# Reciprocals through a DRAM scratch and transposes by DMA, in a two-layer attention and token-MLP kernel on one core

## The chip, the cores and the metric

One Trainium2 chip, one core. The metric is the device time of one execution in microseconds, as the median of several runs. The profile is of one execution, taken by the hardware profiler; its span leaves out a little at both ends.

## The reference

S = 2048 tokens of D = 512 values, bf16. Two layers, each with an attention part A and a token-mixing part B, with the same weights in both layers:

```python
def _A_ref(x, wqkv, wo):            # H = 32 heads of Dh = 16, window W = 256
    qkv = (x @ wqkv).reshape(B, S, 3, H, Dh).transpose(2, 0, 3, 1, 4)
    scores = einsum("bhqd,bhkd->bhqk", q, k) * Dh ** -0.5
    mask = (i - j >= 0) & (i - j < W)
    p = softmax(where(mask, scores, -1e9))
    return einsum("bhqk,bhkd->bhqd", p, v).transpose(0, 2, 1, 3).reshape(B, S, D) @ wo

def _B_ref(x, w1, b1, w2, b2):      # F = 1792; mixes over the tokens
    u = gelu(einsum("bsd,sf->bdf", _layernorm(x), w1) + b1)
    return (einsum("bdf,fs->bds", u, w2) + b2).transpose(0, 2, 1)

x = x + _A_ref(_layernorm(x), wqkv, wo)
x = x + _B_ref(_layernorm(x), w1, b1, w2, b2)
# and both once more
```

## The kernel before

**Tiling.** The 2048 tokens are 16 tiles of 128 rows (`x_sb[:, t]`, t = 0 to 15) and four blocks Q of 512 tokens. The 32 heads are four groups t of eight. A block's attention is 4 groups x 9 steps = 36 steps, so a layer has 144. In each step TensorE makes scores of 64 x 64 cells into one of two pairs of PSUM banks (`emit_scores`, L689), ScalarE takes the exponent (`emit_exp`, L700), VectorE or GpSimd multiplies the edges of the window with a triangle mask (L717), and TensorE multiplies with V (`emit_pv`, L738), which also sums the denominators through two columns of ones. Beside the steps of a block run its own and the next block's projections.

**From x to Q, K, V.** A norm is statistics on VectorE (`ln_stats`, L509 and L510), then `ln_apply`: variance plus epsilon (L517), a pow on GpSimd (L519), the shift (L523), and the scaled tile `xh_sb` on VectorE, ScalarE or GpSimd (L526, L529). `job_transpose` turns a tile of `xh_sb` with four matmuls against the identity into PSUM (L549) and copies it to `xhT` (L433 on VectorE, L435 on ScalarE); `xhT` has two buffers for blocks. `job_k` and `job_q` project (`project`, L560), `job_v` too (L605); `masked` (L570 on VectorE, L575 on ScalarE) copies the result out of PSUM, spread over two masks.

**Denominators.** When a group is done, its outputs and denominators are copied to `oU` and `o2`; after two groups, four small DMAs collect the denominators into `den_c` (one row of 128 for each part of a head), and one larger DMA joins `o2` to `oU`. `job_inverse` takes the reciprocal (L763) and splits it into two bf16 parts `rc2` (L765 to L768). `job_normalise` spreads each reciprocal over the rows of its head with 32 small matmuls against `spread` (L781), two calls for a block, and VectorE multiplies (L788) into `oT`. `job_outproj` multiplies with wo (L654) and adds to x (L658). All this is done for a block while the next block's steps run, and for the last block after the attention.

**B.** `job_part` (L847) and `job_u` (L879) make the hidden layer, gelu on ScalarE (L886); `job_y` (L898) makes one tile of the output and adds it to x (L902), or in the last layer stores it. Most of layer 0's `job_y` runs beside layer 1's attention.

**Order.** Every operation is written down once with its reads and writes; `Plan` derives the waits. The order on each engine is not found at build time: packed tables (`ORDER`, `BANKS`, `LINES`) hold it, so each engine runs its own fixed list and stops at an operation whose inputs are not there. All loads and stores but two go through SyncE's list, also in order; many weight loads wait there for a certain exponent, so that they do not start too early. The costs in the operations were used to make the tables and do nothing at run time.

Of the kernel before, what the change touches and what calls it, by code (L numbers as in the profile page):

```python
# [10 lines left out]
P = 128  # L11
# [17 lines left out]
def _table(*text):  # L29
# [5 lines left out]
    'c-p;`jShq`2!r`}|A)TQnCSkPh09?~oC4CWo!JqbH)hxBetJf`ng_zSzB^KWCUz4<bw1?zP(^V@1hjoFX{LB!YpY$}WrX*L{g9dTE!G)(6{W?M'  # L35
    '{=Ja?K~YUKU36cs_mkwz6jZcU1~NAclX%DtfnKsWV;$C9+@DkPj_>@+4?Xa<j?hPIj3%PZW{uqQCtvU50|dGNd;')
ORDER = _table(
    'c-jrrgMttU00qE@tj)G<d$VoZwz=81ZQHhO+jiZ}M+`s+;b8<rC<I4Hgg_VsAS|LIG$JAj!XXACAsV70GUA{iVj(6XATDAf5#k{}5+E^>A|a9^'
    '1(M((QXv^qA`Ma_EwUpUG9Vo?Av4M%BeEhV(xV8nAUAR#7xEx4@}mIiA`pd96$McUCD0VbPzuFS1|?A%<xl}dQ3+Mh0p(E<)lnI>kPkIb4Rufx'
    'wb32*(HPy(0QJxejnD#3&>XGM8bi<$ZP6ZW&;y;(4xP{uUC<T%&<lMq2|Y0Yz0ntg(H~1O8UryALoo;=5QG^RhEW)fu^5Rl7>_xafT<XV>6nZu'  # L40
    'n2l+eg}IoAnb?PgSb)V?h80+Z<yeI!SdFz<i8a`O`B;a|*o5`iijCNT$Jm11*p6M;i*4A6L)e1@*pI_Ff@3(2qd18ZID@mefKxb+bGU@lxQdIo'
    'g6p`98+e3=xP_azhP$|j+qi@Kcz~z)fR}iICwPYEc#ZFPg?IP}5`2qKc#m)Rj4z1Ig#3Xw$iiRvihuZtzlg&>_>JHU#b6B0kTk<F1j8~S!!Uqi'
    'ct&Lu#$ZfFVmwA;1SViC#$|j)XCfwHWF}@ICSy{jWOAlwYNld3reGRoWLjomX69rzW@1+6V0PwWKIUa^mSG+SGCvEjDvPrqi?J|^upx`GG)u4~'
    'yR#Ncu`J86BFnQfE3g_{uo7#q3hS~u>##N(us)lx5$mxgTeC5nu_;@zGn=y|+p-NiuoDNeJv*`sd$Sw+uq%6U5PPs6d$KPFa2SI)hW$B&LphwI'
    'Ig;}@f}=QrV>yoFIg!&ig_Agyvp9p(Ig<-Hm$SKmOWBT#IiHKTgsZrmD>#{}xr{5hfonO3gSmz~xt=$;k(+p(o4JlRxrNubk9)b5w|Ix!c$c@i'
    'i@Ujl+qs7ad4Oklh^M)qXL*^&d6MUOiYIuEM|hOSc!h^~i5Ga0_j!+xc$H82jL-RsFZh@b`G7C^iBI^JZ}^(;_<^4pO&|H5Klz1U`JKP`jnr@c'
    '<qukM^oPMEg;X&8`#*y)3ZZZct*{EE07X)GMN|aEQ(Q$?WJOUb#Z*+qRt&{bd?iqNB~c<JRAQx5G9_0ErBoW_R6(UyCZ$zAWl=_DP<CZiW@S@S'
    '<y8*lRxagH0Tohy1**6TtB8uJs7k4<N~)YnsEn$pqDrg0DyXU|tEMWcx~i#;YN(!StCs4js~W3;nyS8fsF8ZBxtgez+N-sisjXUSoI0qDI;ovH'
    's-gO*v%0CLx~q#?XpnlTzeZ`G`YA{QG)#jvQhha4BQ!>%HC_`mRTDKyQ#4uAHBGZMQ*$&|GqhY|HD8M~PfN5=L$p}Sv`Q<rMk};b!?jlHwLqJ+'
    'P8+pZTeMnRwO!k^Q#&+EN3}=$v|D?1M7MQNhqXcbbwDR{NT;<+$Mi_YbxId?R_Am@Cv`@bbX6C0U6*xD!F*Hq^jLp&M>q6Pw{%wz^g{RbM$hzG'  # L50
    '&-GIA{YvNcRB!c8pY&Og{ZZfbP4D$Zzf{0KME}!o{ge&=ksQJy{XwA}&Y>LOCko?8j^Kz6?<kJyBo6NAj^S92=Gac<c#h))PUyJK=EM%`<WA~D'
    'PU&Qh>90!R^iJ(GPUj5H;*8GZCQj=z&g#t0?d;Cs>dxa_F6ewN>YUE&LeB3JF5+SibZM7#ahG>tmvUKGaXD9VMOSqNS95(=c1_oC9oKVP*LEW}'
    'a9uZdQ#W)gH+D0(bQ`yDJ9l(z*K!AUa%XpOSGV^7_i%6bba(f1U-xl;_wxu3_8<p&hzEL@hq{}`dbr1Uq$hf`$9tS7c$z1Bl&5&Qr+SWOc#>y&'
    'r4M<j4|=v|`LO4Dp6C0BS9yUK`luKAxR3dSmwAa7d%0J5tyg=ycX*xGc&B%Ho40tY_j<GUd6U<Bk2iXQ_j|Vw__ELXnos(MZ~206`?^p0lCSup'
    'ullA>`;71SoX`7-AN#%^`JwOmfuH%VpZbNL`#%hy?#l')
LINES = {
    "tensor": _table(
    'c-jTQ2fPS$9suzF@BiDz#|qDk(4ms8+^dL-yT_R!XJqdcITE2qR(bY%vNDS2!$bB6Wn}b(%l52{r#zR29QXZ}3Z=s{p-d<n%7tgcUqbm%Ayf>{'
    'g~ae`s1sffZ9@I<Mraq_3mw9g&^9E8&f$YFD@+O#!iOOxObx@r(l9g34-3MguqrGGYr?v)GOP~iVN2K;wukRSM%Wv6hXdhY$OA{i>98mK8P0_x'
    ';Z!&qE``hCdbkm)!=3P3C<V8}&jFx02;_tS3^^bl6oCJQ1SkQ0p)izz3Q!!bhRW~^l!q5!G}MB|FbY~iO=tvfK{IFr9iSsDfUeLJy1-Z%2tA-b'  # L60
    '42BW#F^q$Wunkfm879CSm<m^6HEe-}uncCyd^i9rVJWPI6_5t$a11uV9@q~%U^jdV``|ESzzHZB&%znF1lQpvT!bItF5H8MkOlYQ37i6r7#~C4'
    'm@~#WAr^``VxCwq7K;U9)mSu^jx}Sgm>6G+wPU^bdQ6IqVvE=`Hi>OwgV;W{j_qQv*gKAo$+3Uz7vGIT<2!M991|zUC2>YfiId{gI6JP7v*N<I'
    'EbfhaVroo_i{q;JdCZQF<MX&F?u={V#<(s1Hy(<|Vn#d_55yz!WV{g1$Nlj}ydJaS-S}%f6aS14;=>rwF*7#7+?WdsVqPqbMKA$NVm>U3C9n)u'
    'z*_hsmd8q19joEXSP$!9BKE^Z_!>6AhBzMEU=p^#mbe&uVQcJ)-S9Y0$DTL<2jVE4frD`@4#f#L1k-Q|j=^y_2PflfT#Ko=06)W}xDi+3N?eZz'
    'a2;;NFL4hZ#Qm6wyKx_$#w&OPui>|N3N!E=p2f?UjdxHe3-94Ci1Y-j&?C%Ek&LR6Q!dI&#VLXEQ86k<MW{5DqO$Z71*$|9s0P)c9hgXs=&$q|'
    'HK2y{6xE{+ltj&_BK?R>sXcX~&eVnG(M(!LpVBN^O>3w>&8GD<h|*~)jifP@Lc?eXrO`B6M2l%YEubZ|i8j!ew3en*DjlVrG>5j*Hp-ww^cC%*'
    'uW2uRL&xYUU8KWwf^O3_x<lD?pDs~k<OD9kIoY`gE9d5XJe&)0e$K-+xg=NQ=eaV!#FhB(oXB;#Iyd5p+>Bds9Zuq={5PJ&4Y)J6=Qp_>cjC6('
    'oBMG$?#tadg+JjDJcx(z8XnE#co=`c$vmBB@E%^sb9oM@avJaArM!$+@+wZ}lYEQ!^ESTB$9XRw=7W5U7xQ`k51-~tKF2pWi?8z?e#G}Un}6pA'
    'jFMlTFi9zS%=x6K6qW>ePM(%$rJPigno?0-luA-V21rAxD@pRQyen_WP#G<6N)!2qye;kIpVCs+NoVOH|B{Z<UFyqN=`DlgJ$Xm^NOPGgBV~dt'
    'mnkw`K9UtOS?0+!St7|YR~E}^`9jiVgZwOC%VyakJLR5imqT(;PD_TIk+pJGj>tv1CP(F#T#&0WOK!?f0vc5Gkz`4#xaQVODX6*hDNWEKN?Ke?'  # L70
    'Ybh<KW%YzK)~Z@lt7r{P(&74wHq^XYTNAalHrG1ZL_gB5+Duz%J8iGMw5|5hE;>+q>Hz&lhv-P1s9QBz2kZMfMyKgKovkT4Q^6K!s(z-+^_H&H'
    'G;L`cb(e0}eY!z+>Rvsh8M;_c=><KhS9G%epf@yAuj?Jn(%hD<_w_gZU5nadeWYk&wJnF8(E?W3-16H4{anjhAuDN5TNztwHLS8#u>qE3)h*Fp'
    'v1F@ft*ohavO3np+FA?iZgs7*4Ys$ek9D)&HpoWWF#ETSwlOxxCfayQvAH(NQf;QKx2cwHD{O`>u+_H6mfIJ$&NkW(n_}B-k9}qP?TBr*YxcdJ'
    'vD0?Key|I6-ZJg7J+v&lWA`lEZrTI;#g3c#AIARJZdqRc&T@Hi&*^!*u!ARfB`@ZsynvVX=)L>}ui{m`ns@XO{<e4W_kFbY_Wu5=cl7~Y*ZX*5'
    'Z|L=Xj5qVK-p#xFNFV5ZeVkA9@!rD+`6M6ZvwWU+_78oUPxpmB-#_+GeTjeKvwf-W^UZ$95Bq*k^PRrdclj1y@9BQrPx&ps?l=6Lf9Iz?)3g1q'
    'U-8@ilb`oL{DJ@K5B<LXAER~eNB'),
    "vector": _table(
    'c-jrli&qF{6aeu1-S6J}-OrhZ%A=5XMS13N$}@^$X(h(YW7*EO)-;BRGxJCz;fyo02V%!;Oxv<ep2u;pt#gL340~0|G8whDVXxm`@M{Ml5DM*~'
    '0|Y`#Xam8}7MeqA2!a4;1^uBf^oA(t1N|Tx20#o9f*}wK!(bFlfE0KHl3^T-ha{K?sgMSRuoN<25@bRF3^!|Fgc)iUL%bPjhM67E4NKt=d=5RZ'
# [946 lines left out]
```

## Time and profile before

The runs took 512.4 to 515.64 us, with a median of 514.01. The profiled execution took 514.23 us; its span is 512.1 us.

| | busy us | share of the span |
|---|---|---|
| PE (TensorE matmul) | 481.0 | 94% |
| DVE (VectorE) | 314.1 | 61% |
| ACT (ScalarE) | 323.2 | 63% |
| POOL (GpSimd) | 196.6 | 38% |
| scores L689, PV L738 | 106.5, 90.8 | |
| exponents L700 | 262.8 | |
| transposes L549 (128 matmuls), spread L781 (512) | 11.8, 10.5 | |
| copies of transposes L433, products L788 | 12.4, 20.6 | |

Stages, in us of the span: start to the first score 0 to 17.3; attention of layer 0 to 170.4; B of layer 0 to 243.6; attention of layer 1 to 421.0 (with the rest of layer 0's B in it); B of layer 1 to 512.1. The granted TensorE clock is 1.0 throughout.

How to read it: the chain that ended last goes back from the last instruction, at each step to what released it. A group's line gives line, engine, operation, output and inputs, count, then busy time and mean of one in ns, then the idle time just before and what ended it. In a line of the timeline the first two numbers are the start and the duration in us.

### The profile page before, as it was taken

What the parts mean: (1) busy time and instruction counts of PE and PEld (TensorE: products, weight loads), DVE (VectorE), ACT (ScalarE), POOL (GpSimd) and SP (SyncE); (2) the same over time, 40 slices, a digit from 0 to 9 for tenths busy, and PEclk for the clock granted to TensorE, in tenths of its full rate; (3) what the DMA queues carried; (4) which work ended last, traced back from release to release, by engine and by line L of the source; (5) the groups of instructions that cost most, each with busy time, mean ns of one, the idle gap of its engine ahead of it and who ended that gap; (6) DMA issues with size and microseconds to landing.
All of it is one profiled execution on the core that took longest, in us unless ns stands there. A gap on an engine that the chain in (4) does not pass through costs nothing.

```text
span 512.1 us, 21417 instructions
## 1 busy us (share of the span) xinstructions
PE 481.0 (94%) x9532; PEld 273.9 (53%) x9624; DVE 314.1 (61%) x600; ACT 323.2 (63%) x387; POOL 196.6 (38%) x402
## 2 busy tenths in 40 slices
PE   7889999999999999999899999999899999999997
PEld 3556656665555444445555565666555554444443
DVE  5689878888454661367665764988773754431213
ACT  2989899899999404313678877888888880240000
POOL 5787764856344410010444533664353440100000
PEclk9999999999999999999999999999999999999999
DMA  6192211241121553140003200014213165042632
GB/s 205 47 86 66 69 44 59 78 121 35 36 74 52 157 150 99 47 137 10 4 3 97 86 16 26 4 46 118 76 46 106 47 171 164 12 132 85 193 102 72
DMA packets 70587, 40.71 MB, mean 79 GB/s; under 512 B 7008, under 2 KB 69472, under 8 KB 70496
## 3 DMA queue, kind: packets, MB, share of 16 engines
q1 hardware_dynamic: 66624, 39.33, 26.0%
q0 software_dynamic: 3872, 0.02, 1.5%
q8 instruction: 75, 1.23, 1.0%
q14 instruction: 16, 0.13, 0.1%
HBM read 32.51 MB, written 2.10 MB: 68 GB/s over the span
## 4 chain that ended last, share of the span: by engine, by line
PE 74%; DVE 10%; ACT 7%; issue 4%; POOL 3%; DMA 1%; SPq 0%; POOLq 0%; ACTq 0%; DVEq 0%
PE ps L898 17%; PE ps L689 11%; PE ps L879 11%; PE ps L738 9%; PE ps L560 8%; ACT p_sb L700 5%; PE ps L847 5%; PE ps L605 5%; PE ps L654 4%; DVE stats L509 2%; POOL p_sb L717 1%; PE ps L549 1%; DVE v_all L570 1%; DMA w1buf<-in_B_w_dram 1%; DVE oT L788 1%
## 5 line engine op out<-in xcount | busy, mean ns | idle before, releaser
L700 ACT ACTIVATE p_sb<-ps 128x1024 bf16<-128x1024 f32 (+7 forms) x288 | 262.8, 973 | 41.6 <-PE ps L689 33.9
L717 POOL TENSOR_TENSOR p_sb<-p_sb,edge 128x64 bf16<-128x64 bf16 (+2 forms) x301 | 141.6, 476 | 155.6 <-ACT p_sb L700 129.4
L689 PE MATMUL ps<-q_sb,k_sb 64*64 64x288 bf16 (+8 forms) x2816 | 106.5, 250 | 4.9 <-ACT p_sb L700 2.7
L738 PE MATMUL ps<-p_sb,v_all 64*34 64x288 bf16 (+17 forms) x2816 | 90.8, 245 | 1.7 <-POOL p_sb L717 0.8
L689 PEld LDWEIGHTS ps<-q_sb,k_sb 64*64 64x64 bf16 x2816 | 54.9, 106 | 49.5 <-ACT p_sb L700 25.8
L738 PEld LDWEIGHTS ps<-p_sb,v_all 64*34 64x34 bf16 (+1 forms) x2816 | 59.1, 100 | 14.5 <-POOL p_sb L717 5.1
L898 PE MATMUL ps<-ubuf,w1buf 128*128 128x512 bf16 x266 | 61.9, 379 | 2.7 <-DVE p_sb L717 1.3
L560 PE MATMUL ps<-xhT,wqkv 128*128 128x512 bf16 x214 | 56.5, 380 | 6.7 <-issue 4.6
L902 DVE SCALAR_TENSOR_TENSOR x_sb<-ps,b2col,x_sb 128x512 bf16<-128x512 f32 x32 | 23.7, 750 | 51.9 <-PE ps L898 51.2
L879 PE MATMUL ps<-xh_sb,w1buf 128*128 128x512 bf16 x186 | 43.1, 379 | 1.2 <-issue 0.6
L898 PEld LDWEIGHTS ps<-ubuf,w1buf 128*128 128x128 bf16 x280 | 26.1, 98 | 33.0 <-issue 2.8
L509 DVE BATCH_NORM_STATS2 stats<-x_sb 128x6 f32<-128x512 bf16 x64 | 43.0, 685 | 0.8
L519 POOL TENSOR_TENSOR rstd<-vare,mhalf 128x4 f32<-128x4 f32 x16 | 16.2, 1014 | 69.0 <-DVE vare L517 37.0
L529 ACT ACTIVATE xh_sb<-x_sb,shift,rstd 128x512 bf16<-128x512 bf16 x12 | 9.8, 817 | 48.2 <-POOL shift L523 37.8
L570 DVE TENSOR_TENSOR q_sb<-ps,even 128x1024 bf16<-128x1024 f32 x27 | 32.8, 1216 | 9.2 <-PE ps L560 8.1
L898 PE MATMUL ps<-ubuf,oU 128*128 128x512 bf16 x166 | 38.1, 379 | 0.1
L717 DVE TENSOR_TENSOR p_sb<-p_sb,edge 128x64 bf16<-128x64 bf16 (+2 forms) x99 | 24.4, 249 | 20.1 <-ACT p_sb L700 13.6
L886 ACT ACTIVATE ubuf<-ps,b1col 128x512 bf16<-128x512 f32 x28 | 18.7, 686 | 27.7 <-DVE ps L884 20.2
L570 DVE TENSOR_TENSOR k_sb<-ps,half 128x1024 bf16<-128x1024 f32 x27 | 32.9, 1218 | 5.1 <-PE ps L560 4.7
L605 PE MATMUL ps<-wqkv,xhT 128*32 128x128 bf16 x2048 | 33.9, 220 | 1.1 <-issue 1.1
L570 DVE TENSOR_TENSOR v_all<-ps,even 128x1024 bf16<-128x1024 f32 x26 | 31.6, 1217 | 5.6 <-PE ps L605 5.3
L560 PEld LDWEIGHTS ps<-xhT,wqkv 128*128 128x128 bf16 x256 | 20.6, 97 | 26.5 <-issue 4.2
(70 smaller groups left out, 462.7 us busy)
## 6 DMA issues: line engine op xcount, KB each, us to landing
w1buf<-in_B_w_dram SPq DMA_DIRECT2D x30, 256.0 KB
w1buf<-in_B_w_dram SPq DMA_DIRECT2D x50, 128.0 KB
oU<-in_B_w_dram SPq DMA_DIRECT2D x18, 256.0 KB
oU<-o SPq DMA_DIRECT2D x16, 256.0 KB
w1low<-in_B_w_dram SPq DMA_DIRECT2D x32, 128.0 KB
xhT<-in_B_w_dram SPq DMA_DIRECT2D x4, 512.0 KB
k_sb<-in_B_w_dram SPq DMA_DIRECT2D x4, 512.0 KB
out_dram<-x_sb SPq DMA_DIRECT2D x16, 128.0 KB
```

Of the source, the lines that this page charges most:

```text
L509: dve(lambda e: e.bn_stats(stats[:, t, :], x_sb[:, t, :]), 690, prio, reads=[R("x", t)], writes=[R("stats", t)])
L560: last = e.matmul(ps[:, b, :], lhsT=wqkv[:, c, c0:c0 + P], rhs=xhT[:, buf, c, :], start=(c == 0), stop=(c == 3))
L570: return e.tensor_tensor(dst, src.unsqueeze(2).to_broadcast([P, n, 2, w]), mask[:].unsqueeze(1).unsqueeze(3).to_broadcast([P, n, 2, w]), o ...
L605: last = e.matmul(acc[32 * a:32 * a + 32, k], lhsT=xhT[:, buf, c, t0:t0 + 32], rhs=wv[:, c, :, a, :], start=(k == 0 and c == 0), stop=(k = ...
L689: last = e.matmul(ps[64 * c:64 * c + 64, 2 * half + r, 32 * i0:32 * i1], lhsT=k_sb[rows, ring, t, kb % 16, :], rhs=q_sb[rows, t, c, 32 * i ...
L700: exps[plan.job] = last_exp[0] = plan.op({ACT: (170 + int(2 * (512 - c0) * 0.84), lambda e: e.activation(p_sb[:, slot, :, c0:512], ps[:, 2 ...
L717: return e.tensor_tensor(v, v, g, op=ALU.mult)
L738: last = e.matmul(ps[64 * r:64 * r + w, B_O + (c ^ r), 32 * i0:32 * i1], lhsT=v_all[rows, pos - 32 * c:pos - 32 * c + w], rhs=p_sb[rows, s ...
L847: r = e.matmul(ps[:, b, :], lhsT=w1low[:, fb % 2, sc, (ft % 2) * P:(ft % 2 + 1) * P], rhs=xh_sb[:, sc, :], start=(sc == 0), stop=(sc == 7))
L879: r = e.matmul(ps[:, b, :], lhsT=blk[:, sc - 8 * part, (ft % 2) * P:(ft % 2 + 1) * P], rhs=xh_sb[:, sc, :], start=(sc == 8 * part), stop=( ...
L898: r = e.matmul(ps[:, b, :], lhsT=blk[:, turn[n], (st % 2) * P:(st % 2 + 1) * P], rhs=u_at(turn[n]), start=(n == 0), stop=(n == NFT - 1))
L902: dve(lambda e: e.scalar_tensor_tensor(x_sb[:, st, :], ps[:, b, :], b2col[:, st:st + 1], x_sb[:, st, :], op0=ALU.add, op1=ALU.add), 750, prio,
```

## The change

Eight edits in one:

- For blocks 0 to 2 of each layer the reciprocal (fp32) goes by a DMA to a scratch in DRAM, `recip`, and comes back by four DMAs, `job_scale`, each of which repeats a head's row over its 16 partitions, into one of three buffers `rcb`. VectorE or GpSimd multiplies from there. The last block keeps the matmuls. The rows of `den_c` are in a new order.
- For blocks 1 to 3 of each layer the transposes are DMAs on SyncE's list, straight from `xh_sb` to `xhT`. Block 0 keeps TensorE.
- The first norm is done in two halves of two tiles, with the first x tiles loaded one by one, and its tiles go to VectorE or ScalarE.
- The first K and Q projections of each layer are done in halves of 256 columns.
- The last output tile is computed, added and stored in halves of 256 columns.
- A first exponent on a small tile is run ahead of everything.
- A part of `ln_apply` in layer 0's B gets its own place in the list of jobs.
- New tables, made with some other costs: the whole order on every engine is new. Among others the edge masks on VectorE go from 99 to 141 and on GpSimd from 301 to 259.

```diff
+        recip = nc.dram_tensor("recip", (P, P), dt.float32, kind="Internal").ap()
+        rcb = sb("rcb", [P, NRC, 512], dt.float32)          # NRC = 3
...
-        for t in range(0, 4, 2):
-            load_x(t, t + 2)
+        for t in range(4):
+            load_x(t, t + 1)
...
+        dve(lambda e: e.memset(touch[:], 0.0), 70, -101, writes=[R("touch")])
+        plan.op({ACT: (1480, lambda e: e.activation(touch[:], touch[:], ACTF.Exp))}, reads=[R("touch")], writes=[R("touch")], prio=-101)
...
         def job_transpose(Q, i, prio):
-            b, t, buf = misc_bank(), 4 * Q + i, Q % 2
+            t, buf = 4 * Q + i, Q % 2
+            if Q > 0:
+                plan.op({SP: (1250, lambda e: e.dma_start_transpose(xhT[:, buf, :, i * P:(i + 1) * P], xh_sb[:, t, :]))},
+                        reads=[R("xh", t)], writes=[R("xhT", buf, i)], prio=prio, dma=(1 << 17) + 1)
+                return
+            b = misc_bank()
...
+        def project_halves(Q, which, c0, banks, prio):
+            buf = Q % 2
+            for h, b in enumerate(banks):
+                def f(e, h=h, b=b):
+                    for c in range(4):
+                        last = e.matmul(ps[:, b, 0:256], lhsT=wqkv[:, c, c0:c0 + P], rhs=xhT[:, buf, c, 256 * h:256 * h + 256],
+                                        start=(c == 0), stop=(c == 3))
+                    return last
+                pe(f, 436, prio, reads=[R("wqkv", which)] + [R("xhT", buf, i) for i in (2 * h, 2 * h + 1)], writes=[BK(b)])
...
-                for t in range(2):
-                    todo.append((p0 + NORM0 + 1.4 * t, lambda p, t=t: job_normalise(Q - 1, t, p)))
+                for t in range(4):
+                    todo.append((p0 + NORM0 + 0.7 * t, lambda p, t=t: job_scale(Q - 1, t, p)))
...
             dve(lambda e: e.reciprocal(rc[:], den_c[:]), 930, prio, ...)
+            if Q < NQ - 1:
+                load(recip[:], rc[:], 1 << 16, prio, reads=[R("rc")], writes=[R("recip")])
+                return
...
+        def job_scale(Q, t, prio):
+
+            buf, n = Q % 2, t % NRC
+            row = recip[64 * (t // 2):64 * (t // 2) + 1, :]
+            src = bass.AP(tensor=row.tensor, offset=row.offset + 512 * (t % 2), ap=[[8 * P, 8], [0, DH], [1, 512]])
+            load(rcb[:, n], src, (1 << 18) + 1, prio, reads=[R("recip")], writes=[R("rcb", n)])
+            f = lambda e: e.tensor_tensor(oT[:, buf, t, :], oU[:, buf, t, :], rcb[:, n, :], op=ALU.mult)
+            plan.op({DVE: (640, f), POOL: (1300, f)}, prio=prio, reads=held_o(buf, t) + [R("rcb", n)], writes=[R("oT", buf, t)])
...
+            if last_layer and st == NT - 1:
+                for h, b in enumerate((3, 4)):
+                    cs = slice(256 * h, 256 * h + 256)
...
+                    load(out_v[:, st, cs], x_sb[:, st, cs], 1 << 16, prio, reads=[R("last", h)])
+                return
```

What the new order makes of it, in instructions: matmuls of L549 128 to 32, of L781 512 to 128; copies to `xhT` on VectorE 30 to 6; products into `oT` on VectorE 32 to 25 (17 of them from `rcb`) and 7 on GpSimd; SyncE's list 254 to 311 entries. On ScalarE 10 to 4 K halves, 10 to 4 Q halves and 11 to 4 copies to `o2`; 28 of those on VectorE, where 21 were.

## The prediction

> **What bounds the kernel now.** I read the totals and the chain that ended last, then the busy time by stage, then the waits, then the groups that the change touches. From the page:
>
> ```profile
> PE 481.0 (94%) x9532; PEld 273.9 (53%) x9624; DVE 314.1 (61%) x600; ACT 323.2 (63%) x387; POOL 196.6 (38%) x402
> PE 74%; DVE 10%; ACT 7%; issue 4%; POOL 3%; DMA 1%; SPq 0%; POOLq 0%; ACTq 0%; DVEq 0%
> ```
>
> TensorE is busy for 94% of the span and makes 74% of the chain; DMA has 1% of it. The windows cut at the first and last score matmul of each layer (PE, PEld, DVE, ACT, POOL) show the two attention stages:
>
> ```profile
> 17.30:170.40 153.10, 143.63 (x4098) 91.87 (x4132) 115.64 (x203) 139.68 (x162) 91.63 (x187) 1.00 0.29 69
> 243.60:421.00 177.40, 165.70 (x4190) 101.87 (x4232) 122.82 (x236) 145.49 (x172) 83.21 (x167) 1.00 0.20 58
> ```
>
> In layer 0 TensorE has 94% and ScalarE 91%: two bounds, nearly equal. In layer 1 it is 93% against 82%: TensorE alone. Each layer has 144 score steps, so one takes 153.1/144 = 1.06 us and 177.4/144 = 1.23 us; I use steps as a clock below. The waits of ScalarE in the two stages (total, times, longest) are for TensorE:
>
> ```profile
> ACT p_sb L700 <- PE ps L689: 9.1, 21, 0.8
> ACT p_sb L700 <- PE ps L689: 23.6, 35, 1.9
> ```
>
> **What leaves TensorE.** The groups of the transposes (L549) and of the reciprocal spread (L781), and how they stand in the stream:
>
> ```profile
> L549 PE MATMUL ps<-ident,xh_sb 128*128 128x128 bf16 x128 | 11.8, 220 | 2.6 <-ACT xh_sb L529 1.2 <-ACT v_all L575 0.7 <-ACT xhT L435 0.6
> L781 PE MATMUL ps<-rc,spread 64*64 64x128 bf16 x512 | 10.5, 218 | 0.8 <-DVE rc L768 0.4 <-issue 0.3
> ```
>
> ```profile
> 346.75 0.39 PE L549 MATMUL ps<-ident,xh_sb 128*128 128x128 bf16 x4
> 347.06 0.42 PE L689 MATMUL ps<-q_sb,k_sb 64*64 64x64 bf16 x12
> ```
>
> 24 of the 32 calls of four transposes go, and 12 of the 16 calls of 32 spread matmuls. A transpose call is busy for 11.8/32 = 0.37 us; the next work starts 0.31 us after it here. A spread call is busy for 0.65 us; between neighbours of its own kind the next starts 0.45 us later, so I take 0.5. That is 24 x 0.37 = 8.9 and 12 x 0.5 = 6.0 us, 14.9 in all, half in each attention stage: 7.4 each. In layer 1, where nothing else is near the bound, I count 6.5 of 7.4. In layer 0 ScalarE limits: by the two orders its own list shrinks by one masked V pair (2 x 0.69), two norm applies (2 x 0.82) and takes 1.0 us more of copies, 2.0 us less in all, and the rest can only come out of its waits. I take the middle of 2.0 and 7.4: 4.7.
>
> **VectorE and GpSimd** get no longer, so they cost nothing: VectorE loses 24 copies of 415 ns (10.0), 24 products from PSUM at 0.68 against 17 from SBUF at about the same (4.8), and takes 42 more edge masks of 0.25 (10.5) and 7 copies of 0.68 (4.8): about zero, at 75% and 69% busy in the two stages. GpSimd gives the 42 masks away (20 us) and takes 7 products, which no row shows: between 0.43 us (a quarter of the size) and four times that, 12 us at most.
>
> **What is added on SyncE's queue**: 24 transposing DMAs, 6 stores of the reciprocals (64 KB) and 24 loads of 256 KB. Rows for a DMA's price, from the timeline and the queues:
>
> ```profile
> 173.93 1.29 SPq L427 DMA_DIRECT2D den_c<-o  x2
> 176.66 0.95 DVE L763 RECIPROCAL rc<-den_c 128x128 f32<-128x128 f32 x1 [1.23 <-DMA den_c<-o]
> ```
>
> ```profile
> q1 hardware_dynamic: 66624, 39.33, 26.0%
> q0 software_dynamic: 3872, 0.02, 1.5%
> ```
>
> Issue takes about 0.6 us, and the last tiny DMA had landed 176.66 - 175.22 = 1.44 us later. A packet costs 0.26 x 512.1 x 16/66624 = 32 ns of one engine, whether it carries 590 bytes (first row) or 5 (second). So 57 more DMAs (three of them from the loads and stores that are split) of 0.6 us add 34 us to a queue whose long rows are gated waits: hidden, as long as what they bring is not late.
>
> *Transposes.* Not in this trace. Low end: a plain 128 KB, 256 packets of 512 bytes, 0.5 us. High end: cut into 32-byte pieces (16 rows of two bytes), 4096 x 32 ns/16 = 8.2 us (cut into single elements it would be 131 us; I leave that out as no use at all). I take 1 us of transfer and 2 us to land, nearest to the plain load of the same size. By the new order, from the issue of a block's set to the first use of its last member there are, in layer 0, 12 steps for four (12.7 us), 12 for three (12.7) and 15 for four (15.9); in layer 1, 16 (19.7), 18 (22.1) and 12 for four (14.8). All are covered, so cost 0. What covers them is that the norms of a block are finished a block ahead. Behind a transpose that waits for its norm on SyncE stand weight loads, whose uses come a stage later.
>
> *Reciprocals.* From the reciprocal to the first product: issue 0.6, land 1.44, issue 0.6, 256 KB at 18.5 GB/s (590 bytes in 32 ns) on 16 engines 0.89, land 1.44: 5.0 us. The new order leaves 6, 5 and 5 steps in layer 0 (6.4, 5.3, 5.3) and 5, 5 and 6 in layer 1 (6.2, 6.2, 7.4). It just fits; cost 0, but thin. The waiting product stands on VectorE (17) or GpSimd (7) ahead of copies out of PSUM and of edge masks, for which TensorE waits. The load's source has an outermost dimension of 8; if only 8 engines move it, 0.89 becomes 1.77 and the two gaps of 5.3 are missed by 0.6 each. The Trainium skill says just that ("DMA: Bandwidth & Descriptors", Rules for kernel authors: the slowest dimensions set how many engines take part, so an outermost dimension under 16 confines the DMA to that many); no run here shows it. By it the forecast is about 1 us longer.
>
> **Start.** The change loads ScalarE's table early, halves the first norm, K and Q, and puts V behind them:
>
> ```profile
> 8.67 1.28 ACT L529 ACT_TABLE_LOAD   x1 [8.67 <-POOL shift L523]
> ...
> 15.99 1.26 ACT L575 ACTIVATE q_sb<-ps,even 128x512 bf16<-128x512 f32 x2
> ...
> 18.28 1.90 ACT L700 ACTIVATE p_sb<-ps 128x960 bf16<-128x960 f32 x2
> ```
>
> The table's 1.28 us goes from the path. Of the halved norm I expect little, since the second half's pow (1.0 us on GpSimd) follows the first's. The first score now waits for two V calls on TensorE (1.04 each) and two Q masks on VectorE (0.65 each) side by side, where three ScalarE pairs of 1.26 stood in a row; but the first exponent still stands behind two V pairs on ScalarE. Bounds: 1.0 (the table, less two more matmul fills) to 3.5 (table, one V call and one mask). I take 2.0.
>
> **End.** The last output in halves shortens the 0.75 us of VectorE behind the last matmul to 0.41 by its halved columns, and the last store by at most 0.2:
>
> ```profile
> 508.93 0.02 issue
> 508.95 0.75 DVE x_sb L902
> ```
>
> Its 28 matmuls of 256 columns take what 14 of 512 took. I take 0.5.
>
> **Sum.** 2.0 + 4.7 + 6.5 + 0.5 = 13.7 us off the profiled execution's 514.2 (span 512.1, 2.1 around it; the median of the runs is 514.0): 500.5.
>
> **Rivals.** *(a) ScalarE bounds both stages*: its own lists shrink by 2.0 in each. For: 91% in layer 0, and the score slots tie the two engines together. Against: 82% in layer 1, with 23.6 us of waits for TensorE. With the start and the end as above: 514.2 - 2.0 - 2.0 - 2.5 = 507.7.
>
> *(b) The transposes are late: slower.* With T per transpose, one after another, the sets are late by what 4T (or 3T) exceeds the gaps above. At 8.2 us: 20.1 + 11.9 + 16.9 + 13.1 + 10.7 + 18.0 = 91, so 591. TensorE would stand at the V matmuls (L605 before) behind them. It decides from about T = 4.7, where the lateness eats the 13.7. For: 32 ns per packet however small. Against: nothing says that the pieces are that small. The Trainium skill ("VectorE: DVE Perf Modes", The three transpose paths) has 1309 ns for 128x128 by DMA against 390 ns on TensorE; the trace has four in 0.39 us busy on TensorE, and no DMA one. If four squares followed one another, 5.2 us, an estimate, the lateness would be 25 us and the time 525; if they overlap, nothing changes.
>
> *(c) The reciprocals are late*: each chain takes 8 us in place of 5.0. Late by 1.6 + 2.7 + 2.7 + 1.8 + 1.8 + 0.6 = 11, so 512. For: six serial chains through DRAM, margins of 0.3 us. Against: 4 to 6 steps lie between most products and their output projection.
>
> *(d) The new table leaves new holes* as large as the work removed: 514.
>
> **Chances.** Forecast 0.55, (a) 0.14, (b) 0.13, (c) 0.13, (d) 0.05. A measurement of this kernel tells about 1%, 5 us. Faster by more: the forecast, most of (a) and a little of (c), 0.70. Within: the rest of (a), half of (c) and of (d), 0.12. Slower: (b) and what is left, 0.18. Low end 489: the full 7.4 in both stages, 3.5 at the start, the 3.4 us of idle time in front of the two groups, and some of VectorE's waits behind them (7.1 at L433, 8.4 at L788). High end 522: (a), (c), (d), and (b) just past its deciding point. The forecast by itself: 492 to 507.
>
> **What would show it.** Right: first exponent at about 16.3; attention stages of about 148 and 171 us; 4 spread calls and 8 transpose calls; no PE wait for a DMA into xhT above 1 us. Wrong: V matmuls released by xhT's DMA (b); VectorE idle before the product with rcb (c); ScalarE at 95% in both stages (a). The forecast fails if layer 1 shortens by under 3 us.

## The result and the profile after

The kernel after takes 527.24 us (527.03 to 528.04, four runs), the kernel before 513.49 (512.4 to 515.64) beside it: a ratio of 1.0265, interval 1.0229 to 1.0302. It is slower by 13.7 us where I forecast 13.7 us faster: 26.7 us above the 500.5 and 5.2 above the high end of the range. The profiled execution took 528.04 us, its span is 526.3.

The page of the kernel after, totals of the engines, chain that ended last by engine and by line:

```profile
PE 475.6 (90%) x9081; PEld 265.7 (50%) x9174; DVE 323.5 (61%) x623; ACT 317.1 (60%) x377; POOL 182.0 (35%) x361
...
PE 65%; DMA 12%; DVE 6%; issue 6%; ACT 6%; POOL 3%; SPq 2%; DVEq 0%; ACTq 0%; POOLq 0%
PE ps L964 17%; PE ps L930 11%; PE ps L728 9%; DMA rcb<-recip 8%; PE ps L777 7%; PE ps L571 6%; ACT p_sb L739 5%; PE ps L693 4%; PE ps L644 4%; PE ps L898 3%; DMA recip<-rc 2%; SPq L429 2%; DMA w1low<-in_B_w_dram 1%; PE ps L507 1%; POOL p_sb L756 1%
```

The share of DMA in the chain has gone from 1% to 12%, and the second line says which: 8% are the loads of the reciprocals, 2% their store. TensorE's share fell from 74% to 65%. Its busy time fell by 5.4 us only, though the removed calls were counted as 14.9. The kernel of experiment 1, which has the same matmuls without the waits and a clock of 1.0 throughout, is busy for 471.8 us, so 3.8 us of the difference goes with the lower clock (last section). Scores and products with V, as many as before, are busy for 2.1 and 2.4 us longer there (108.6 and 93.2 against 106.5 and 90.8); why is not shown.

The work did leave as planned. The groups of transposes and of the spread, after (x is the count, then busy time):

```profile
L560 PE MATMUL ps<-ident,xh_sb 128*128 128x128 bf16 x32 | 2.6, 220 | 0.8 <-DVE xh_sb L532 0.8
L832 PE MATMUL ps<-rc,spread 64*64 64x128 bf16 x128 | 2.6, 219 | 1.3 <-DVE rc L810 0.9 <-DVE oT L839 0.4
```

The windows of the two attention stages after (columns as in the prediction; here a stage runs from the start of its first score matmul to the start of its last, and the prediction's later cuts lie 1.5 to 3.9 us behind these):

```profile
14.97:179.03 164.06, 140.04 (x3857) 85.83 (x3892) 120.83 (x221) 137.33 (x159) 82.87 (x167) 0.99 0.44 91
253.08:432.67 179.59, 161.74 (x3906) 95.58 (x3940) 122.43 (x234) 140.57 (x163) 77.17 (x145) 0.98 0.29 79
```

Stages cut in this way, in us:

| | start | attention, layer 0 | between | attention, layer 1 | end |
|---|---|---|---|---|---|
| before | 17.3 | 151.1 | 73.8 | 174.9 | 95.0 |
| after | 15.0 | 164.1 | 74.1 | 179.6 | 93.6 |

So start and end shortened (2.3 and 1.4), and both attention stages, where 11.2 us should have been won, grew by 13.0 and 4.7. The waits of the two multiplying engines (total, times, longest) and of ScalarE:

```profile
ACT p_sb L739 <- PE ps L728: 65.1, 65, 6.0
...
DVE oT L819 <- DMA rcb<-recip: 28.7, 15, 3.6
POOL oT L819 <- DMA rcb<-recip: 14.0, 6, 6.0
```

21 of the 24 products wait for their load, 42.7 us in all. One block's chain in the timeline shows how (start, duration, engine and line, released by):

```profile
64.08 0.95 DVE L802 RECIPROCAL rc<-den_c 128x128 f32<-128x128 f32 x1 [0.56 <-DMA den_c<-o]
...
65.28 0.53 SPq L429 DMA_DIRECT2D recip<-rc  x1
...
69.64 1.31 SPq L429 DMA_DIRECT2D rcb<-recip  x2
...
72.25 0.60 SPq L429 DMA_DIRECT2D rcb<-recip  x1
...
73.75 0.69 DVE L819 TENSOR_TENSOR oT<-oU,rcb 128x512 bf16<-128x512 f32 x1 [2.99 <-DMA rcb<-recip]
...
76.17 0.68 DVE L819 TENSOR_TENSOR oT<-oU,rcb 128x512 bf16<-128x512 f32 x1
...
76.94 0.61 SPq L429 DMA_DIRECT2D rcb<-recip  x1
...
82.06 0.69 DVE L819 TENSOR_TENSOR oT<-oU,rcb 128x512 bf16<-128x512 f32 x1 [1.23 <-DMA rcb<-recip]
...
83.22 0.81 PE L693 MATMUL ps<-wo_sb,oT 128*128 128x512 bf16 x3 [0.85 <-DVE oT L819]
```

The reciprocal ends at 65.03, the first product starts 8.7 us later and the fourth 17.0 us later; in the six blocks 6.5 to 8.7 us (mean 7.5) and 14.2 to 17.0 (mean 15.7). The fourth load reuses a buffer, and so is issued only when the product that reads it is done: here the second product (76.17 + 0.68), which itself stands behind a mask and a copy on VectorE; in the six blocks it is twice the first, three times the second and once the third, and the load follows it by 0.1 to 0.4 us. The output projection starts 0.47 us after the last product (82.06 + 0.69 to 83.22), and TensorE had waited 0.85 us for it.

### The profile page after: what moved, and what is told of

Read it like the earlier page. It is cut to its first block, busy times and chain, and to the rows that moved or that the text cites. A ratio compares the mean times of both kernels' runs of the same rounds, so it can differ in the third digit from the quotient of the medians.

```text
span 526.3 us, 20596 instructions
## 1 busy us (share of the span) xinstructions
PE 475.6 (90%) x9081; PEld 265.7 (50%) x9174; DVE 323.5 (61%) x623; ACT 317.1 (60%) x377; POOL 182.0 (35%) x361
## 4 chain that ended last, share of the span: by engine, by line
PE 65%; DMA 12%; DVE 6%; issue 6%; ACT 6%; POOL 3%; SPq 2%; DVEq 0%; ACTq 0%; POOLq 0%
PE ps L964 17%; PE ps L930 11%; PE ps L728 9%; DMA rcb<-recip 8%; PE ps L777 7%; PE ps L571 6%; ACT p_sb L739 5%; PE ps L693 4%; PE ps L644 4%; PE ps L898 3%; DMA recip<-rc 2%; SPq L429 2%; DMA w1low<-in_B_w_dram 1%; PE ps L507 1%; POOL p_sb L756 1%
## 5 line engine op out<-in xcount | busy, mean ns | idle before, releaser
L756 POOL TENSOR_TENSOR p_sb<-p_sb,edge 128x64 bf16<-128x64 bf16 (+2 forms) x259 | 121.1, 473 | 174.5 <-ACT p_sb L739 135.1
L728 PE MATMUL ps<-q_sb,k_sb 64*64 64x288 bf16 (+8 forms) x2816 | 110.0, 252 | 5.3 <-issue 2.9
L777 PE MATMUL ps<-p_sb,v_all 64*34 64x288 bf16 (+17 forms) x2816 | 94.4, 248 | 13.0 <-DVE p_sb L756 7.6
L777 PEld LDWEIGHTS ps<-p_sb,v_all 64*34 64x34 bf16 (+1 forms) x2816 | 59.4, 101 | 31.4 <-DVE p_sb L756 10.8
L756 DVE TENSOR_TENSOR p_sb<-p_sb,edge 128x256 bf16<-128x256 bf16 (+2 forms) x141 | 40.3, 296 | 22.2 <-ACT p_sb L739 19.9
L525 POOL TENSOR_TENSOR rstd<-vare,mhalf 128x4 f32<-128x4 f32 (+1 forms) x17 | 16.8, 986 | 74.4 <-DVE nmean L527 54.9
L591 DVE TENSOR_TENSOR k_sb<-ps,half 128x1024 bf16<-128x1024 f32 (+1 forms) x30 | 35.3, 1177 | 7.8 <-PE ps L571 4.2
L591 DVE TENSOR_TENSOR q_sb<-ps,even 128x1024 bf16<-128x1024 f32 (+1 forms) x32 | 36.5, 1147 | 5.2 <-PE ps L728 2.8
L898 PE MATMUL ps<-xh_sb,w1low 128*128 128x512 bf16 x110 | 29.4, 387 | 7.0 <-DMA w1low<-in_B_w_dram 4.4
L964 PE MATMUL ps<-ubuf,oU 128*128 128x512 bf16 x150 | 34.5, 379 | 0.2
L644 PEld LDWEIGHTS ps<-wqkv,xhT 128*32 128x32 bf16 x2048 | 29.6, 98 | 6.8 <-issue 3.5
```

Of the source, the lines that this page charges most:

```text
L591: return e.tensor_tensor(dst, src.unsqueeze(2).to_broadcast([P, n, 2, w]), mask[:].unsqueeze(1).unsqueeze(3).to_broadcast([P, n, 2, w]), o ...
L644: last = e.matmul(acc[32 * a:32 * a + 32, k], lhsT=xhT[:, buf, c, t0:t0 + 32], rhs=wv[:, c, :, a, :], start=(k == 0 and c == 0), stop=(k = ...
L728: last = e.matmul(ps[64 * c:64 * c + 64, 2 * half + r, 32 * i0:32 * i1], lhsT=k_sb[rows, ring, t, kb % 16, :], rhs=q_sb[rows, t, c, 32 * i ...
L756: return e.tensor_tensor(v, v, g, op=ALU.mult)
L777: last = e.matmul(ps[64 * r:64 * r + w, B_O + (c ^ r), 32 * i0:32 * i1], lhsT=v_all[rows, pos - 32 * c:pos - 32 * c + w], rhs=p_sb[rows, s ...
L898: r = e.matmul(ps[:, b, :], lhsT=w1low[:, fb % 2, sc, (ft % 2) * P:(ft % 2 + 1) * P], rhs=xh_sb[:, sc, :], start=(sc == 0), stop=(sc == 7))
```

## The experiments

My theory after the result: C, the chain through DRAM is late, and VectorE and GpSimd, standing at the products, hold back masks and copies for which TensorE waits. Rivals: S, the queue of SyncE and the transposes on it; O, the new order. All ratios below are to the kernel before in runs on the same chip; differences in us are of medians, and the ratios give the same within about 1 us. The profiles are of single executions, and a stage that two kernels have in common differed by up to 4 us between them, so small sums rest on the medians.

**1. No wait for the reciprocals.** All DMAs stay; the product no longer reads what they bring.

```diff
-  e.tensor_tensor(oT[:, buf, t, :], oU[:, buf, t, :], rcb[:, n, :], op=ALU.mult)   # reads rcb
+  e.tensor_tensor(oT[:, buf, t, :], oU[:, buf, t, :], oU[:, buf, t, :], op=ALU.mult)
```

> The changed kernel, but the 24 products multiply each output by itself in place of the broadcast reciprocals (so the normalisation is left out), and so wait for no load; all stores, loads and transposes are still issued at their places. Theory C (the reciprocals' trip through DRAM is late, and VectorE and GpSimd stand 42.7 us in front of the products with edge masks and copies queued behind them): the whole loss goes, 527 to about 500, between 497 and 506. Rival O (the new written order and the moved edge masks lose the time): 518 to 527. Rival S (SyncE's queue or the DMA traffic itself costs): 518 to 527, since both stay.

514.13 us, ratio 1.000 (0.9976 to 1.0024), in the gap between the ranges I had given. So 13.1 us of the loss are the waits, half of the 26.7; C is right as far as it goes and does not go far enough. The wait that passed from the products to ScalarE shrinks with it, and layer 1's attention takes 168.67 us in place of 179.59, layer 0's 158.42 in place of 164.06:

```profile
ACT p_sb L739 <- PE ps L728: 49.6, 60, 6.0
```

```profile
248.33:417.00 168.67, 158.36 (x3905) 94.28 (x3938) 122.84 (x234) 140.28 (x163) 75.79 (x145) 1.00 0.30 84
```

**2. What makes the chain slow.** First a fourth buffer, in the room of `rc` and `rc2`; then the source of the loads with 16 in its outermost dimension, for which the reciprocals are stored twice; then both.

```diff
-  NRC = 3
+  NRC = 4
```

```diff
-  ap=[[8 * P, 8], [0, DH], [1, 512]]
+  ap=[[8 * P, 16], [0, DH // 2], [1, 512]]     # each row of 8 stored twice, so 2 stores
```

> The changed kernel with four buffers for the broadcast reciprocals in place of three (the room is won by taking the reciprocal in place and by keeping the last block's split reciprocals in the first buffer). The fourth load of a block then need not wait for the first product. Theory C: the fourth product comes about 6 us earlier in each of six blocks; it makes about half of the wait, so 527 becomes 512 to 519. Rivals O and S: 525 to 527.

> The changed kernel with the scratch stored twice, so that the slowest dimension of each broadcast load's source is 16 and not 8 (one more 64 KB store per block). If the slowest dimension sets how many DMA engines move a load, a load's packets take about 1.1 us in place of 2.1, and theory C gives 519 to 524 (the first product 1 us, the third 3 us earlier, the store 0.4 us later). If not, packets still take 2.1 us a load and the time is 527 to 530.

> Both the scratch stored twice (16 rows a load) and four buffers. Theory: of the 13 us that the reciprocals' trip costs, 10.4 went with 16 rows and 2.8 are left; the fourth load's wait for a buffer is most of that: 514 to 516. Rival (four loads at once only share the engines): 516.5 to 518.

Four buffers: 526.05 (1.0233; 1.0195 to 1.0272), 1.2 us and not clear of noise, where I expected 8 to 15. The edit frees the fourth load less than I thought, since SyncE's list keeps its order: it follows the third by 0.6 to 5.1 us, where it was 3.2 to 7.2. Sixteen rows: 516.88, ratio 1.006 (1.0028 to 1.0091), 10.4 us, more than I expected. Both: 518.22 (1.0089), no better than sixteen rows alone. The waits with sixteen rows:

```profile
DVE oT L821 <- DMA rcb<-recip: 15.5, 10, 3.4
POOL oT L821 <- DMA rcb<-recip: 9.0, 5, 3.5
```

24.5 us in place of 42.7, although there is one more store for each block (this execution took 522.2, above the median of its kernel). The packets in the two traces agree: a load is 128 packets of 2,048 bytes, each of some 88 ns (84 with 16 rows); with 8 rows there are most often 8 under way at once, with 16 most often 16. A load that runs alone takes 1.7 to 2.1 us with 8 in five of seven cases (3.3 and 3.8 in the others) and 1.2 to 1.7 with 16 in five of seven (2.3 and 2.4 in the others); three that run together take 6.2 to 7.1 with 8 and 3.5 to 4.4 with 16. That is what the Trainium skill says ("DMA: Bandwidth & Descriptors", Rules for kernel authors: an outermost dimension under 16 confines the DMA to that many engines), and the trace agrees: 8 and 16 in flight, worth 10.4 us here.

**3. The transposes.** In the order of before, with nothing else of the change; then the kernel of experiment 1 without them.

```diff
+  if Q > 0:      # before's order otherwise
+      plan.op({SP: ... e.dma_start_transpose(xhT[:, buf, :, i * P:(i + 1) * P], xh_sb[:, t, :])}, ...)
+      return
```

```diff
-  plan.op({SP: ... e.dma_start_transpose(...)}, ...)      # experiment 1, Q > 0
   return
-  b, buf = misc_bank(), Q % 2                             # K, Q and V projections
+  b, buf = misc_bank(), 0
```

> The kernel before, with its own order and tables, and one part of the change: the 24 sets of four transposes outside the first blocks go from TensorE and VectorE to DMA. TensorE sheds 24 x 0.37 = 8.9 us and VectorE 24 copies of 0.42 us. Theory C (this part is sound and the loss is all in the reciprocals): 505 to 510, against 513.5 before. Rival S (transposing DMAs hold SyncE's queue 1.2 us each, ahead of the loads that gather the denominators, or land late): 514 to 520.

> The kernel whose products wait for no load (514.1 us), and without the 24 transposing DMAs: all blocks project the transposed input of the first block. Theory S (the transposing DMAs, 1.2 us of SyncE's queue each and a landing that V waits for, cost the time that is still missing): 503 to 509. Rival O (the order of the rest costs it; transposes by DMA are hidden): 512.5 to 515.

The first took 529.6 (1.0284), above both ranges. In the old order some V matmuls stand soon behind a tile's norm, and here TensorE waits for the DMAs:

```profile
302.25 5.20 SPq L544 DMA_TRANSPOSE xhT<-xh_sb  x4
304.80 1.15 PEld L608 LDWEIGHTS ps<-wqkv,xhT 128*32 128x32 bf16 x64 [4.42 <-DMA xhT<-xh_sb]
...
PE ps L608 <- DMA xhT<-xh_sb: 8.2, 3, 4.2
```

One transpose holds SyncE's queue for mostly 1.2 to 1.3 us (four: 5.20) and is there 2.55 us after its issue began (302.25 to 304.80); the other two that TensorE waits for, the second and third of their sets, take 4.1 and 3.5. The second took 509.09 (505.6 to 513.87 in four runs), ratio 0.9891 (0.9844 to 0.9938), 5.0 us less than with the transposes, though no wait for `xhT` in the kernel after exceeded 0.9 us. So they cost about 5 us (3 to 8 by the intervals). The two profiles have 5.0 us of their difference in layer 0's attention (158.42 against 153.38) and 0.5 in layer 1's (168.67 against 168.18):

```profile
14.58:167.96 153.38, 137.93 (x3856) 84.73 (x3890) 119.75 (x221) 136.95 (x159) 83.17 (x167) 1.00 0.35 87
```

How (the queue, or contention with other transfers) was not separated.

**4. The new order.** With no written order at all, each engine's list is found at build time; so for both kernels.

```diff
-  LINES = { ... }
+  LINES = {}
```

> The kernel before without its written order: the planner in the kernel orders the five engines by its own costs and due times. A control for the next run: slower than 514, perhaps 520 to 545.

> The changed kernel without its written order, by the same planner. Rival O (the new written order is worse made than the old one): the changed kernel is then not slower than the planned kernel before, a ratio of 0.97 to 1.00. If the change itself costs the time, as under the reciprocals' and the transposes' trips: slower by 2 to 5%.

554.93 and 558.28 us, two runs each. The one to the other is 1.006, between the two ranges, where the written orders give 1.0265: under one and the same planner the change costs little, and gains nothing either. That speaks for O, but weakly: both kernels are 31 to 41 us slower than with their written orders, and other waits may hide a loss.

**5. Mending the order by hand.** The first starts from sixteen rows and puts the two small bias loads on GpSimd, which stand ahead of an edge mask in the first steps, behind layer 0's attention. The others start from the first: one moves three masked copies from VectorE to ScalarE in steps 9 to 36, one divides the edge masks between VectorE and GpSimd as before from step 9 on, one puts 11 products 1 to 4 instructions later.

```diff
-  GpSimd:   load b2col, mask, load b1col, mask, ...          # the first
+  GpSimd:   mask, mask, ... , load b2col, load b1col
-  VectorE:  product (waits for rcb), mask, copy, ...         # the last
+  VectorE:  mask, copy, product, ...
```

> The kernel with the scratch stored twice (16 rows a load, 516.9 us), and in GpSimd's list the two small bias DMAs moved from step 9 to GpSimd's idle times at about 161 and 177 us. Theory G: in the changed kernel GpSimd stood 3.2 us ahead of the first of these DMAs, an edge mask stood behind it, TensorE was idle for 2.8 us, and the 3.4 us after that ran at half clock; without that 512.5 to 515. Rival: the stall only moves, or the time is made up later: 516 to 518.

> As the run with the late bias DMAs, and three masked copies of layer 0's first block (at about 36, 47 and 53 us) go from VectorE (1.2 us each) to ScalarE (two of 0.7). Theory V: VectorE, 91 to 93% busy in steps 9 to 36 of the changed order against 88% before, sets the pace there; 1 to 2.5 us less than that run. Rival: ScalarE's exponents, behind the copies, then set the pace: no change or up to 1.5 us more.

> The kernel with 16 rows a load and late bias DMAs (516.6 us), and from step 9 on the edge masks divided between VectorE and GpSimd as in the kernel before: 100 go from VectorE to GpSimd, 65 the other way. Theory M: in the changed kernel masks stand on VectorE behind 1.2 us copies and behind products, and TensorE waits for them (18.4 us in front of the P V matmuls by VectorE's masks, none by them before the change): 3 to 7 us less, 509.5 to 513.5. Rival Q (the masks are only where a wait shows; what is late is the reciprocals' trip): 515 to 519.

> The kernel with 16 rows a load and late bias DMAs (516.6 us); 11 of the 24 products stand one to four instructions later in the lists of VectorE and GpSimd, behind edge masks and copies that had waited behind them. Theory C: the 27.5 us of waits in front of the products fall to about 12, and the time to 514 to 515.5. Rival: the output projections, half a microsecond behind the last product in half of the blocks, come later: 516.5 to 519.

516.55, 516.44, 523.31 and 527.94: nothing, nothing, and two losses. The last is of use. VectorE's waits for the loads fell, and TensorE's output projections waited for the products in their place:

```profile
DVE oT L821 <- DMA rcb<-recip: 10.1, 10, 1.8
...
PE ps L693 <- POOL oT L821: 3.9, 1, 3.9
PE ps L693 <- DVE oT L821: 2.7, 2, 2.0
```

So these products stand about as late as the output projection lets them; moving them later moved the wait to TensorE.

**6. SyncE's queue.** The gather of denominators, the store and the first three loads put ahead of transposes and weight loads; then this with the masks divided as before (experiment 5).

```diff
-  SyncE: store, weights, transpose, load, load, transpose, load, transpose, ...
+  SyncE: store, store, load, load, load, weights, transpose, transpose, transpose, ...
```

> The kernel with 16 rows a load and late bias DMAs (516.6 us), with another order on SyncE's queue alone: in five of the six blocks the gathers of the denominators, the store of the reciprocals and the first three broadcast loads go ahead of transposes and weight loads that stood between them. Theory Q: transposes hold the queue 1.2 us each; in layer 1 the gathers stood behind three and four of them and the reciprocal came 3.7 us late; the products' waits (27.5 us) halve: 511 to 514. Rival M (masks): 515.5 to 517.

> Both: masks divided as before, and the gathers, store and loads first on SyncE's queue. If each of the two theories holds, the gains add: 506 to 511. If only one, the time is that one's.

544.54 (1.0596) and 552.17 (1.0731). The timeline of the first, SyncE's queue:

```profile
63.93 1.23 SPq L429 DMA_DIRECT2D recip<-rc  x2
67.89 2.79 SPq L429 DMA_DIRECT2D rcb<-recip  x3
...
71.36 3.87 SPq L552 DMA_TRANSPOSE xhT<-xh_sb  x3
```

The loads must wait until the stores have landed, and the queue stands from 65.16 to 67.89 with everything that is behind them. What is late next shows in the waits:

```profile
PE ps L900 <- DMA w1low<-in_B_w_dram: 10.7, 2, 6.6
...
PE ps L644 <- DMA xhT<-xh_sb: 5.0, 2, 4.0
```

The order as given had other transfers between store and loads, and that was better.

**7. All reciprocals by the spread on TensorE, in the new order.**

```diff
-  todo.append((p0 + NORM0 + 0.7 * t, lambda p, t=t: job_scale(Q - 1, t, p)))
+  todo.append((p0 + NORM0 + 0.7 * t, lambda p, t=t: job_normalise(Q - 1, t, p) if t < 2 else None))
```

> The changed kernel with the reciprocals of all blocks spread on TensorE again (12 calls of 32 matmuls, products from PSUM on VectorE, no scratch and no broadcast loads); transposes by DMA, halves and the written order of the rest stay. Theory: the order without any wait for reciprocals takes 514.1, and this adds some of the 6.0 us of spread calls: 515 to 520. Rival (only the reciprocals' part does harm, and transposes by DMA with the halves bring their 7 to 9 us): 505 to 510.

539.2 us (1.0495). TensorE stood 0.7 to 1.8 us ahead of eight of the twelve spread calls at the places where I put them, mostly for copies on VectorE and ScalarE. This judges my placement and not the part, and I draw nothing from it.

**8. What TensorE's time is worth.** The kernel before, in its own order, without the twelve transpose calls and copies of one layer.

```diff
+  if Q > 0 and prio < 300:      # layer 0; prio > 300 for layer 1
+      return
   b, t, buf = misc_bank(), 4 * Q + i, Q % 2
```

> The kernel before, with its written order kept, without the twelve transpose calls and their twelve copies for blocks 1 to 3 of layer 0, and nothing in their place: those blocks project the first block's transposed input again, so the output is that of other inputs. It leaves TensorE 12 x 0.37 = 4.4 us and VectorE 12 x 0.415 = 5.0 us less to do in that stage; ScalarE's list is the same. Theory S (ScalarE and the two score slots bound the attention of layer 0, so time taken from TensorE there comes back as idle time): 512.5 to 514, and the stage stays within 1 us of 151.1. Theory T (TensorE bounds it too, and what the change loses there is only waits of its own): the stage shortens by 3.5 to 4.5, 509 to 510.

> The same in layer 1 alone: twelve transpose calls and their copies less, layer 0 as before. Both theories have TensorE alone as the bound there: the stage of 174.9 shortens by 3.5 to 4.5, 509 to 510.5 in all. If it too stays, the removed calls stood in idle time in both layers, and my term of 6.5 us for layer 1 was right for another reason.

511.55, ratio 0.9955 (0.9936 to 0.9974), for layer 0; 510.29, 0.9926 (0.99 to 0.9953), for layer 1; 513.25 before. 4.4 us of TensorE work bring 1.7 (by the ratio 2.3; interval 1.3 to 3.3) and 3.0 (3.8; 2.4 to 5.1). I go by the ratios: about half of the time in layer 0 and most of it in layer 1. The copies on VectorE go with the calls (5.0 us in each layer), so this is the worth of both together. Neither theory of layer 0 was right; it lies between them, as the forecast had taken it. The profile of the first warns of single executions:

```profile
18.39:170.83 152.44, 138.72 (x4041) 88.12 (x4076) 109.94 (x188) 138.06 (x160) 89.80 (x184) 1.00 0.28 66
244.58:415.61 171.03, 162.70 (x4211) 100.69 (x4244) 120.94 (x230) 142.87 (x168) 80.60 (x161) 1.00 0.19 55
```

Layer 0, which lost work, is 1.4 us longer than in before's profile, and layer 1, where nothing was changed, 3.9 us shorter.

**9. The change in layer 1 alone.** Layer 0 and its order as before; from the end of layer 0's B the order after, with transposes by DMA, reciprocals by DMA from sixteen rows, layer 1's first K and Q in halves, and the last output in halves.

```diff
-  if Q > 0:                       # transposes by DMA
+  if Q > 0 and prio > 300:
...
-  if Q < NQ - 1:                  # reciprocals by DMA
+  if Q < NQ - 1 and prio > 300:
```

> Layer 0 as in the kernel before, with its order; from the end of layer 0's MLP on as in the kernel with 16 rows a load: transposes and reciprocals by DMA in layer 1 alone, last output in halves. Theory (layer 1's attention is limited by TensorE alone and gains what the waits leave of 6 us, the end gains 1.4, and layer 0 has nothing to give): layer 1's attention 171 to 173 us in place of 174.9, the whole 509 to 512 against 514.1 of the kernel before. Rival (the gain of layer 1 needs the state in which the new layer 0 leaves the engines): 513 to 516.

509.54 us, ratio 0.9907 (0.988 to 0.9933): 0.9% under the kernel before. Its layer 1 (170.93 us long) and its waits for reciprocals:

```profile
244.10:415.03 170.93, 164.23 (x3943) 94.48 (x3940) 121.88 (x234) 140.24 (x163) 76.57 (x145) 1.00 0.31 84
```

```profile
DVE oT L817 <- DMA rcb<-recip: 8.5, 7, 3.0
POOL oT L817 <- DMA rcb<-recip: 6.8, 5, 3.9
```

The products still wait 15.3 us in its three blocks. The evidence is the ratio, 4.8 us by it; the stage's length alone would not do, since an unchanged layer 1 took 171.03 in experiment 8. About 1.4 of the 4.8 is the end (508.7 - 415.03 us, before 512.1 - 417.06), where the last output in halves is, so some 3.4 are left for the rest.

## Why the prediction was wrong

The miss of 26.7 us is made of the waits for reciprocals, 13.1 (experiment 1; 10.4 of it by the rows, experiment 2), the transposes, about 5.0 (experiment 3), and 8.6 that are left when neither stands in the way (509.09 - 500.5).

- **The step that failed first: "Reciprocals … 5.0 us … It just fits; cost 0, but thin."** Measured 7.5 us on average to the first product, and the gaps of 5.3 to 7.4 us could not hold that. Each part of the sum was too short. From the reciprocal to the end of the store's issue it took 0.85 us on average, where I had 0.6; from there to the first load 2.2, where I had 1.44 (3.8 in the block shown, with other transfers in between); and from that load's issue to the first product 4.4, where I had 2.9. I priced one load; three share 8 engines, and the fourth follows a product, so that the last product comes 15.7 us behind the reciprocal. I had the right rule ("if only 8 engines move it") and sized it at 1 us: it was worth 10.4. I put it on the first product alone, not on a train of four.
- **"Against: 4 to 6 steps lie between most products and their output projection"**, in rival (c), was true of the first products and not of the last: in three of the six blocks the projection starts 0.3 to 0.8 us after the last product (83.22 above, and at 121.5 and 416.3). (c) was the right mechanism, with a chance of 0.13, and its 8 us for each chain were near the 7.5; but it charged 11 us for six chains, where the waits cost 13.1, and left the gain of 13.7 whole.
- **"Transposes … All are covered, so cost 0."** No V matmul waited long for one, as I said, so (b) did not come about in the kernel after; in the old order it did (529.6). But the 24 DMAs cost about 5.0 in all. They hold SyncE's queue for 1.2 us each, where I had 0.6; that this is the cause is not shown. In (b), the lateness at 5.2 us each comes to about 23 us by the gaps given there, not 25.
- **"VectorE and GpSimd get no longer, so they cost nothing."** VectorE's busy time rose by 9.4 us (314.1 to 323.5), not by about zero: the edge masks took 15.9 more (40.3 against 24.4), where I had 10.5, and the copies of Q and K that left ScalarE 6.1 more (71.8 against 65.7), which the sum left out. GpSimd's fell. And a product that stands waiting blocks the masks behind it: `PE ps L777 <- DVE p_sb L756` is 7.6 us of waits after, and none of that kind is left in experiment 1.
- **TensorE's worth: 4.7 of 7.4 in layer 0, 6.5 of 7.4 in layer 1**, that is 64% and 88%. Experiment 8 has 2.3 and 3.8 of 4.4, 52% and 86%. These terms were about right; that the change lost is not because TensorE's time was worth nothing (rival a; ScalarE is busy for 84 and 78% of the two stages after, not 95). Once the waits are gone, layer 1's attention takes 168.67 us (experiment 1), and 168.4 was forecast (174.9 - 6.5), though single profiles of that stage differ by up to 4 us.
- **Start and end: -2.0 and -0.5.** First exponent forecast at about 16.3, measured 16.49 (before 18.28); the end shortened by 1.4. But the start's gain was gone by exponent 9, counted from 0 (30.66 against 28.47). With the bias loads moved (first kernel of experiment 5) exponent 9 starts at 26.28, and yet exponent 36 at 53.95, against 53.34 before.
- **The signs I named.** 4 spread calls and 8 transpose calls, and no long wait of TensorE for `xhT`: so it was. VectorE idle before the product with `rcb`, the sign of (c): so it was, 28.7 us. Layer 1 had to shorten by 3 us at least; it grew.
- **The 8.6 us left.** By the profile most of it is in layer 0's attention, 153.4 us in the second kernel of experiment 3, where 146.4 were forecast (151.1 - 4.7). Its first block, exponents 0 to 36, takes 38.06 us there (16.10 to 54.16) and 35.06 before, though neither reciprocals nor transposing DMAs stand in its way; VectorE is busy for 33.99 of it, 30.56 before. From there to the last score it is only 1.2 shorter than before (113.8 against 115.0). That execution was 3.5 us under the median of its kernel, so the place is not sure. Experiment 8 explains 0.9 of it (12% of 7.4). That the rest is in the new order of layer 0, as in rival (d), is only argued; moving masks, copies and small loads (experiment 5) did not find it. It stays open.

## What to carry to other kernels

A round trip through DRAM has to be priced for the whole train that shares it: the last load, behind the others, sets the consumer's time, and each landing that a queue waits for stands in front of what is behind it. Count the outermost dimension of a broadcast source; eight rows here cost 10 us that two stores mended. And look first at the stage where the freed engine is the bound: in layer 1 alone the edits with sixteen rows win 0.9%, the halved last output included, and in both layers they lose 0.6%. That the bound makes this difference is argued, since layer 0 got a new order too.

## What the runs showed of the hardware

**A short stall can cost TensorE twice.** The granted clock of the kernel after changes in steps of 3.41 us. Three times it falls to half for one such step, each time behind a step in which TensorE was busy for a third or less. Windows of the kernel after (second, fourth and sixth follow the first, third and fifth; PE busy after the length, granted clock third from the end), and one in which TensorE was busy for half and the clock stayed:

```profile
22.96:26.37 3.41, 0.50 (x16) 0.26 (x10) 1.48 (x4) 1.24 (x3) 2.37 (x3) 1.00 0.69 155
26.37:29.78 3.41, 3.39 (x67) 1.87 (x69) 1.86 (x3) 1.14 (x2) 2.54 (x7) 0.50 2.52 118
316.51:319.92 3.41, 1.03 (x5) 0.61 (x7) 2.68 (x5) 1.21 (x3) 1.15 (x1) 1.00 0.15 54
319.92:323.33 3.41, 3.41 (x34) 1.53 (x33) 0.94 (x2) 0.79 (x1) 2.06 (x3) 0.50 0.16 53
408.67:412.08 3.41, 1.11 (x56) 0.88 (x48) 0.87 (x2) 2.18 (x3) 0.67 (x1) 1.00 0.68 177
412.08:415.49 3.41, 3.00 (x39) 1.49 (x44) 1.41 (x4) 1.02 (x1) 0.43 (x1) 0.50 0.54 113
...
152.72:156.13 3.41, 1.69 (x51) 1.00 (x46) 1.15 (x2) 2.27 (x3) 0.67 (x1) 1.00 0.60 156
```

So 15, 30 and 33% busy were followed by half the clock here, and 50% was not. The limit is not sharp: in the trace of the last kernel of experiment 5 steps of 41 and 42% were followed by the full clock, in that of the sixteen rows one of 44% by half. Each half step can cost up to 1.7 us beyond the stall (an estimate, half of 3.41); the profiled executions of the kernel before and of experiment 1 have none within the span. The Trainium skill ("TensorE: Matmul & The Clock Gate", Part 1: The HAM clock gate) states the half clock after an idle window of about 3.4 us; these windows were 15 to 33% busy, not idle.

**GpSimd stood 3.2 us before its first small DMA**, with an edge mask behind it, for which TensorE waited 2.77 us (in the kernel before GpSimd stood 1.1 us there):

```profile
23.96 1.38 POOL L1015 DMA_DIRECT2D b2col<-in_B_b_dram  x1 [3.16 <-issue]
...
25.87 0.32 PE L777 MATMUL ps<-p_sb,v_all 64*34 64x288 bf16 x4 [2.77 <-POOL p_sb L756]
```

Moving it away (experiment 5) did not change the median: 516.55 against 516.88.
